# Moving value, weight and key/query loads of a fused attention + MLP kernel to earlier slots

## The chip, the cores and the metric

One core of a Trainium2 chip. Its engines are PE (TensorE, with its weight loads shown apart as PEld), DVE (VectorE), ACT (ScalarE), POOL (GpSimd) and SP (SyncE, which only issues transfers). They run side by side, each through its own instructions in order, and wait for each other by semaphores. The metric is the device time of the whole program in microseconds (us), the median of several runs.

## The reference

Attention over 8 batches of 8 heads, 576 rows, 64 columns, and then a two-layer MLP over the 4608 rows of 512:

```python
scores = scale * np.matmul(q, k.transpose(0, 1, 3, 2))
thresh = np.max(scores, axis=-1, keepdims=True) - tau
scores = np.where(scores >= thresh, scores, -1000000000.0)
attn = np.exp(scores - max); attn = attn / (sum + 1e-09)
x = matmul(attn, v), heads side by side, as (4608, 512)
h = x @ w_in                       # 512 x 2048
out = (h * np.clip(h + 3.0, 0.0, 6.0) / 6.0) @ w_out   # 2048 x 512
```

(max and sum are those of the row; the last lines of the attention are put together here.)

## The kernel before

**Tiling.** Two heads make a pair and two pairs a *quad*; there are 16 quads, two per batch. A quad has 9 *slots*: eight of 128 query rows of one pair (both its heads), and one that takes the last 64 rows of both pairs. The loop of L527 runs over the 144 slots n; quad q has slots 9q to 9q + 8. Each pass n works on several slots at once (a pipeline written out by hand), and each engine takes the pass's work in the order of the code:

- `scores(n+2)` (L277): PE makes q times k into PSUM, for both heads.
- `sm_max(n+1)` (L294): DVE copies scores out of PSUM and takes the row maximum (L302); POOL turns it into the mask's bias (L305).
- `sm_mask`, `sm_exp` (L307, L312): ACT applies the threshold (L309) and the exponential with row sum (L314). Up to slot N1 = 22 the exponential of slot n-1 stands ahead of the mask of slot n.
- `sm_recip(n-1)` (L316): DVE takes the reciprocal of the row sums (L317).
- `sm_norm(n-1)` (L319): POOL scales the rows to bf16 (`pn`, L322). They are transposed either by PE (`pe_transpose`, L337, two passes later, for the slots marked `on_chip`: slots before 21 with number 1, 3, 5, 7 or 8 in their quad, and number 0 from quad 1 on), or by a DMA transpose that SP issues (L330).
- `multiply(n)`: PE multiplies transposed rows with values (L346, L349). From slot 22 on PE also has the MLP's two matmuls (L381, L415), with ACT (L389) and DVE (L391, L404) between them.

PE also has filler: transposes of the identity (`warm_up`, L185), 17 at the start, some more in the lead-in, and 8 + 6 per pass in passes 0 to 7.

**Loads.** `load_quad(quad)` (L82) allocates a quad's tiles from a pool of three buffers (L49) and appends its transfers as jobs to the list `loads`. For the first two batches (quads 0 to 3) these are five jobs: keys of pair 0, queries of pair 0, remainders (last 64 rows of keys and queries, four transfers), keys of pair 1, queries of pair 1, all issued by SP (except the first queries, by ACT). From quad 4 on there are four jobs: queries 0, keys 0, queries 1, and `both`, which is the key remainders and keys 1. These transfers are cut into 32-row blocks, four per job, issued by SP; the key remainders are issued by POOL:

```python
(nc.sync if b < NB else nc.gpsimd).dma_start(out=dst[64 * n:64 * n + 64, :]...   # L126, n = 0, 1
```

`load_v(b)` (L138) appends a batch's value transfers to `vcasts` (two of four heads each and two remainders for batches 0 and 1), and `load_weights` (L161) appends 16 pieces of w_in and then 16 of w_out to `casts`; POOL issues these, since they change f32 into bf16 on the way.

**When they are issued.** `start(jobs, n)` (L171) pops and issues up to n jobs. Quad 0 is issued ahead of everything (L176). The others come at the end of each pass, behind `sm_norm` (L618 to L625): first one job of `loads` in most passes, then either one of `vcasts` or one or two of `casts`, by the pass's number. L535 says in which pass a quad's jobs are appended to `loads`.

**The lead-in** (L452 to L480) is the work before the loop: PE transposes the first keys (L232) and queries (L458 to L461), and makes the scores of slots 0 and 1; DVE and POOL make the maximum and the bias of slot 0.

Of the kernel before, what the change touches and what calls it, by code (L numbers as in the profile page):

```python
# [9 lines left out]
F32 = mybir.dt.float32  # L10
# [5 lines left out]
P = 128  # L16
# [4 lines left out]
def kernel(  # L21
# [10 lines left out]
    nc = tc.nc  # L32
# [15 lines left out]
    singles = ctx.enter_context(tc.tile_pool(name="singles", bufs=1))  # L48
# [20 lines left out]
    nat = {}  # L69
# [6 lines left out]
    loads = []  # L76
    casts = []
    vcasts = []
# [59 lines left out]
    def load_v(b):  # L138
        vm = v_pool.tile([P, H, 4 * D], BF16, tag="vm", name="vm")
        vr = vrs[b % 2]  # L140
        vsb[b] = (vm, vr)
        w = 4 if b < NB else 2
        mains = [lambda h=h: nc.gpsimd.dma_start(  # L143
            out=vm[:, h:h + w, :], in_=v[b, h:h + w, 0:512, :].rearrange("h (p t) d -> p h (t d)", t=4))
            for h in range(0, H, w)]
        rests = [lambda a=a: nc.gpsimd.dma_start(
            out=vr[a * 64:(a + 1) * 64, a, :, :],
            in_=v[b, :, 512:S, :].rearrange("(hp a) p d -> a p hp d", a=2)[a]) for a in range(2)]
        vcasts.extend(mains + rests if b < NB else mains[0:1] + rests + mains[1:])
# [21 lines left out]
    def start(jobs, n):  # L171
        for _ in range(min(n, len(jobs))):
            jobs.pop(0)()
# [9 lines left out]
    def warm_up(count):  # L183
        for _ in range(count):
            nc.tensor.transpose(ps[:, HB, 0:P], identf[:], identf[:])  # L185

    warm_up(17)
    identb = singles.tile([P, P], BF16)
    nc.vector.tensor_copy(out=identb[:], in_=identf[:])
    three = singles.tile([P, 1], F32)  # L190
# [103 lines left out]
    def sm_max(sl):  # L294
        sl.s = s_pool.tile([P, 2, S], F32, tag="s", name="s")
        sl.m = stat_pool.tile([P, 2], F32, tag="m", name="m")
        sl.bias = stat_pool.tile([P, 2], F32, tag="bias", name="bias")
        sl.rsum = stat_pool.tile([P, 2], F32, tag="rsum", name="rsum")
        sl.rinv = stat_pool.tile([P, 2], F32, tag="rinv", name="rinv")
        for i in range(2):  # L300
            c0 = score_col(sl.n, i)
            nc.vector.tensor_scalar(out=sl.s[:, i, :], in0=ps_flat[:, c0:c0 + S],  # L302
                                    scalar1=1.0, scalar2=None, op0=Alu.mult, op1=Alu.max,
                                    accum_out=sl.m[:, i:i + 1])
        nc.gpsimd.tensor_scalar(out=sl.bias[:], in0=sl.m[:], scalar1=-scale, scalar2=tau, op0=Alu.mult, op1=Alu.add)  # L305

    def sm_mask(sl, i):  # L307
        s = sl.s[:, i, :]
        nc.scalar.activation(out=s, in_=s, func=Act.Prelu, bias=sl.bias[:, i:i + 1], scale=scale,  # L309
                             alpha=REJECT)  # L310

    def sm_exp(sl, i):  # L312
        s = sl.s[:, i, :]
        nc.scalar.activation(out=s, in_=s, func=Act.Exp, accum_out=sl.rsum[:, i:i + 1])  # L314

    def sm_recip(sl):  # L316
        nc.vector.reciprocal(out=sl.rinv[:], in_=sl.rsum[:])  # L317
# [54 lines left out]
    def mm1(item, hb=HB):  # L372
        b, ni, c0 = item
        if c0 is None:
            for ki in range(KI):
                nc.tensor.matmul(ps[:, hb, :], xR[b // 2][:, ki, :], w_in_sb[:, ki, ni * P:ni * P + 512],  # L376
                                 start=(ki == 0), stop=(ki == KI - 1))
        else:
            for n in range(2):
                for ki in range(KI):  # L380
                    nc.tensor.matmul(ps[:, hb, n * 256:(n + 1) * 256], w_in_sb[:, ki, (ni + n) * P:(ni + n + 1) * P],  # L381
                                     xT[b][:, ki, c0:c0 + 256], start=(ki == 0), stop=(ki == KI - 1))
        return ps[:, hb, :]
# [122 lines left out]
    def multiply(n):  # L506
        copies = []
        for of, pair, *columns in products.get(n, ()):
            copies.append(av_rest(of) if pair is None else av_main(pair, *columns))
            if of % 2 and pair is None:  # L510
                todo1.extend(moe_of(of // 2)[1])
            elif pair == 2 * of + 1 and of % 2 and columns[0] == 0:
                todo1.extend(moe_of(of // 2)[0])
        return copies

    def second():
        nonlocal pieces, bb, mt, part
        pieces = 2 if now % 2 == 0 and todo2 else 0
        for _ in range(pieces):
            bb, mt, part = todo2.pop(0)  # L520
            mm2_part(bb, mt, part)
# [5 lines left out]
    for n, sl in enumerate(queue):  # L527
        quad, slot = sl.quad, sl.slot
        b, g = divmod(quad, 2)
        now = n  # L530
        if slot in (0, 4):
            pts[2 * quad + slot // 4] = pt_pool.tile([P, 9, 512], BF16, tag="pT", name="pT")
        if slot == 8:
            ptr[quad] = ptr_pool.tile([P, 9, P], BF16, tag="pR", name="pR")
        for ahead in {0: (1, 2), 9: (3,), 16: (4,)}.get(n, (quad + 2,) if quad > 2 and slot == (2 if quad == 3 else 0) else ()):  # L535
            if ahead < NQUAD:
                load_quad(ahead)
        if slot == 0 and g == 1 and b + 1 < B:
            load_v(b + 1)
        for copy in last_keys:  # L540
            copy()
        last_keys = []
        if 0 < n <= N1:
            for i in range(2):
                sm_exp(prev, i)
        if n + 1 < len(queue):
            sm_max(queue[n + 1])
        even = n >= N1 and n % 2 == 0
        if n > N1:
            sm_recip(prev)  # L550
        for copy in waiting:
            copy()
        waiting = []

        if todo1:
            item, then = todo1.pop(0)
            if n == len(queue) - 2:
                second()
            h = mm1(item, 0 if n == len(queue) - 1 else OB if n > N1 and n % 2 and not pieces else HB)
            todo2.extend(then)  # L560
        else:
            item = None
        if n >= N1:
            for copy in multiply(n):
                copy()
        if item:
            mm1_gate(item, h, mm1_relu(h, on_act=even))
        copies = pe_transpose(queue[n - 2]) if n > 1 and queue[n - 2].on_chip else None
        if prev is not None and n < N1:
            sm_recip(prev)  # L570
        if copies:
            copies()
        if n != len(queue) - 2:
            second()
        if n <= N1:
            for i in range(2):
                sm_mask(sl, i)
        if n == N1:
            sm_recip(prev)
        if n >= N1:  # L580
            for i in range(2):
                sm_exp(sl, i)
            if n + 1 < len(queue):
                for i in range(2):
                    sm_mask(queue[n + 1], i)
        if n < N1:
            for copy in multiply(n):
                copy()
        if part == 3:
            waiting.append(lambda tile=(bb, mt): late.extend(mm2_out(*tile, on_act=False)))  # L590
            part = 0
        evict = []
        for job, of in turns.get(n, ()):
            if job == "k":
                (last_keys if even else evict).append(transpose_k(of))
            elif job == "q":
                if of // 2 not in qkT:
                    alloc_qk(of // 2)
                (waiting if even else evict).append(transpose_q(of))
            else:  # L600
                (last_keys if even else evict).append(transpose_rest(of, of_k=of > 0))
        for out_of_psum in evict:
            if out_of_psum:
                out_of_psum()
        if n == 0:
            warm_up(8)
        if n <= N1:
            scores(n + 2)
        elif n % 2:
            for m in (n + 3, n + 2):  # L610
                if m < len(queue):
                    scores(m)
        if n < 8:
            warm_up(6)
        if n > 0:
            sm_norm(prev)
        flush()
        if n == 0:  # L618
            start(loads, 2)
        elif n not in (4, 12, 15, 18, 21) and not 23 < n < 30 and (n < 37 or n % 2 == 0):  # L620
            start(loads, 1)
        if n < 4 or 15 < n < 20 or n > 33:
            start(vcasts, 1 if n < N1 or n % 2 else 0)
        else:
            start(casts, 2 if n in (5, 8, 11, 14) or 21 < n < 28 else 1)  # L625
        prev = sl
# [82 lines left out]
```

## Time and profile before

| what | value |
|---|---|
| median of 8 runs | 520.68 us (519.96 to 521.04) |
| the profiled execution | 520.73 us, span 519.0 us |
| PE busy | 503.6 us, 97% of the span |
| DVE, ACT, POOL busy | 442.6, 452.1, 299.3 us |
| DMA | 78.77 MB, mean 152 GB/s |
| queue q1 (SP's transfers) and q0 (POOL's), share of 16 engines | 77.3% and 15.2% |
| lead-in, up to the first mask on ACT | 10.8 us |

The span is what lies between the first and the last instruction on record; the time is what the device took for the program. Times inside the profile count from the span's start. A pass is found in the trace by POOL's bias (L305): the first of its 144 lies in the lead-in, and the k-th after it in pass k - 1. So passes 0 to 21 lie at 10.8 to 76.6 us, and the steady stage, in which two passes take some 6.3 us together, begins near 116 us. Idle time in front of an instruction is given in square brackets, with what ended it; "issue" means that the profile shows nothing that it waited for.

### The profile page before, as it was taken

The numbers are of one execution on the slowest core, as the hardware profiler recorded it, in microseconds if no ns is written. First come the engines' busy times: TensorE is split into PE (matmuls) and PEld (weight loads), VectorE is DVE, ScalarE is ACT, GpSimd is POOL, SyncE is SP. The second block draws the span as 40 slices with busy tenths as digits, with TensorE's granted clock in tenths as the row PEclk, the third lists the DMA queues.
The fourth block names the chain that finished last, engine by engine and source line by source line (L and its number), as shares of the span: only waits on it lengthen the run. The fifth ranks groups of instructions, "written<-read, shape, count | busy, mean of one in ns | idle before, by whom it ended". The sixth has DMA issues, their size and how long they took to land.

```text
span 519.0 us, 12068 instructions
## 1 busy us (share of the span) xinstructions
PE 503.6 (97%) x4089; PEld 321.8 (62%) x4145; DVE 442.6 (85%) x1124; ACT 452.1 (87%) x980; POOL 299.3 (58%) x538
## 2 busy tenths in 40 slices
PE   8999899999999999999999999999999999999997
PEld 6765555666665666666665666666665666667563
DVE  3788887998999999999999999999999999887261
ACT  3999979999999999999999999999999999987060
POOL 0787869756676666657566656657566655552000
PEclk9999999999999999999999999999999999999999
DMA  5799899989999999999999999999999997564222
GB/s 131 111 176 167 138 157 162 171 150 174 166 175 156 166 171 161 171 161 175 174 157 188 155 192 169 163 168 176 168 155 185 178 177 122 117 112 70 78 66 61
DMA packets 314094, 78.77 MB, mean 152 GB/s; under 512 B 296624, under 2 KB 309168, under 8 KB 314032
## 3 DMA queue, kind: packets, MB, share of 16 engines
q1 hardware_dynamic: 294464, 67.90, 77.3%
q0 software_dynamic: 18368, 9.71, 15.2%
q8 instruction: 32, 0.52, 0.5%
q10 hardware_dynamic: 1200, 0.39, 0.3%
q14 instruction: 30, 0.25, 0.1%
HBM read 36.70 MB, written 9.44 MB: 89 GB/s over the span
## 4 chain that ended last, share of the span: by engine, by line
PE 80%; ACT 3%; DVE 2%; issue 1%; POOL 0%; POOLq 0%
PE ps L287 25%; PE ps L415 23%; PE ps L381 21%; PE ps L346 6%; PE ps L376 3%; ACT s L314 1%; PE ps L349 1%; ACT s L309 1%; DVE g L404 1%; ACT r L389 1%; DVE s L302 0%; DVE r L391 0%; POOL pn L322 0%; PE ps L257 0%; ACT kT L222 0%
## 5 line engine op out<-in xcount | busy, mean ns | idle before, releaser
L322 POOL TENSOR_SCALAR pn<-s,rinv 128x576 bf16<-128x576 f32 x288 | 210.6, 743 | 19.9 <-issue 4.5
L302 DVE TENSOR_SCALAR_CACHE_REDUCE s<-ps 128x576 f32<-128x576 f32 x288 | 205.0, 749 | 17.6 <-PE ps L287 9.0
L309 ACT ACTIVATE s<-s,bias 128x576 f32<-128x576 f32 x288 | 205.8, 763 | 6.0 <-POOL bias L305 5.7
L314 ACT ACTIVATE s<-s 128x576 f32<-128x576 f32 x288 | 192.5, 671 | 0.3
L287 PE MATMUL ps<-kT,qT 64*128 64x384 f32 (+7 forms) x1280 | 174.0, 419 | 4.7 <-DVE s L302 3.8
L287 PEld LDWEIGHTS ps<-kT,qT 64*128 64x128 f32 (+1 forms) x1280 | 103.6, 175 | 59.3 <-issue 15.8
L381 PE MATMUL ps<-xT,w_in_sb 128*128 128x256 bf16 x1024 | 130.9, 273 | 0.2 <-DVE g L404 0.2
L415 PE MATMUL ps<-w_out_sb,g 128*128 128x512 bf16 x524 | 123.7, 379 | 2.8 <-issue 0.2
L381 PEld LDWEIGHTS <-w_in_sb 128*128 128x128 bf16 x1024 | 95.5, 98 | 40.0 <-issue 20.8
L305 POOL TENSOR_SCALAR bias<-m 128x2 f32<-128x2 f32 x144 | 26.9, 187 | 154.3 <-DVE rinv L317 137.1
L404 DVE SCALAR_TENSOR_TENSOR g<-r,ps 128x512 bf16<-128x512 f32 x128 | 87.8, 687 | 15.1 <-ACT r L389 11.1
L415 PEld LDWEIGHTS <-g 128*128 128x128 bf16 x576 | 56.2, 98 | 56.8 <-issue 0.4
L389 ACT ACTIVATE r<-ps,three 128x512 f32<-128x512 f32 x81 | 55.6, 687 | 27.9 <-PE ps L381 23.8
L314 ACT ACTIVATION_READ_ACCUMULATOR s<-s 128x1 f32 x288 | 54.5, 189 | 0.0
L391 DVE TENSOR_SCALAR r<-ps 128x512 f32<-128x512 f32 x63 | 42.9, 681 | 0.0
L346 PE MATMUL ps<-pT,vm 128*64 128x256 bf16 (+1 forms) x480 | 39.1, 285 | 0.0
L346 PEld LDWEIGHTS <-vm 128*64 128x64 bf16 x736 | 27.2, 110 | 16.0 <-issue 14.3
L357 DVE CAST xT<-ps 128x256 bf16<-128x256 f32 (+1 forms) x60 | 26.2, 437 | 11.8 <-PE ps L349 11.8
L423 DVE TENSOR_SCALAR osb<-ps 128x512 f32<-128x512 f32 x31 | 20.9, 673 | 8.4 <-PE ps L415 8.4
L302 DVE DVE_READ_ACCUMULATOR s<-ps 128x1 f32 x288 | 23.9, 83 | 0.0
L317 DVE RECIPROCAL rinv<-rsum 128x2 f32<-128x2 f32 x144 | 23.0, 160 | 0.6 <-ACT s L314 0.6
L143 POOL DMA_DIRECT2D vm<-in_v_dram x28 | 21.4, 766 | 0.7 <-issue 0.7
(57 smaller groups left out, 260.5 us busy)
## 6 DMA issues: line engine op xcount, KB each, us to landing
out_dram<-osb SPq DMA_DIRECT2D x31, 256.0 KB, 3.4
nq<-in_q_dram SPq DMA_DIRECT2D x96, 72.0 KB, 3.5
km<-in_k_dram SPq DMA_DIRECT2D x96, 64.0 KB, 3.1
vm<-in_v_dram POOLq DMA_DIRECT2D x24, 128.0 KB, 4.1
km<-in_k_dram SPq DMA_DIRECT2D x16, 128.0 KB, 3.5
w_in_sb<-in_moe_w_in_dram POOLq DMA_DIRECT2D x16, 128.0 KB, 3.6
w_out_sb<-in_moe_w_out_dram POOLq DMA_DIRECT2D x16, 128.0 KB, 3.9
pT<-pn SPq DMA_TRANSPOSE x117, 3.8
```

What stands on the lines that cost most here:

```text
L287: nc.tensor.matmul(ps_flat[rows, c0:c0 + w], qT_of(pair)[a * 64:(a + 1) * 64, q0:q0 + rows.stop - rows.start], kT_of(pair)[a * 64:(a + 1) ...
L302: nc.vector.tensor_scalar(out=sl.s[:, i, :], in0=ps_flat[:, c0:c0 + S], scalar1=1.0, scalar2=None, op0=Alu.mult, op1=Alu.max, accum_out=sl ...
L305: nc.gpsimd.tensor_scalar(out=sl.bias[:], in0=sl.m[:], scalar1=-scale, scalar2=tau, op0=Alu.mult, op1=Alu.add)
L309: nc.scalar.activation(out=s, in_=s, func=Act.Prelu, bias=sl.bias[:, i:i + 1], scale=scale, alpha=REJECT)
L314: nc.scalar.activation(out=s, in_=s, func=Act.Exp, accum_out=sl.rsum[:, i:i + 1])
L322: nc.gpsimd.tensor_scalar(out=pn[:, i, :], in0=sl.s[:, i, :], scalar1=sl.rinv[:, i:i + 1], scalar2=1.0, op0=Alu.mult, op1=Alu.mult)
L346: nc.tensor.matmul(pb[a * 64:(a + 1) * 64, :], vm[:, 2 * hp + a, c * D:(c + 1) * D], pT[:, 5 * a + c, cols], start=(c == 0), stop=False)
L381: nc.tensor.matmul(ps[:, hb, n * 256:(n + 1) * 256], w_in_sb[:, ki, (ni + n) * P:(ni + n + 1) * P], xT[b][:, ki, c0:c0 + 256], start=(ki = ...
L389: nc.scalar.activation(out=r, in_=hps, func=Act.Relu, bias=three[:])
L391: nc.vector.tensor_scalar(out=r, in0=hps, scalar1=3.0, scalar2=0.0, op0=Alu.add, op1=Alu.max)
L404: nc.vector.scalar_tensor_tensor(out=out, in0=r, scalar=6.0, in1=hps, op0=Alu.min, op1=Alu.mult)
L415: nc.tensor.matmul(o_ps[0], gbuf[:, ni, mt * P:(mt + 1) * P], w_out_sb[:, ni, :], start=(ni == 0), stop=(ni == NI - 1))
```

## The change

```diff
     warm_up(17)
+    landed = singles.tile([P, 1], F32)
+    nc.gpsimd.tensor_copy(out=landed[:], in_=nat[0][1][:, 0, 1, 0:1])
+    start(vcasts, 2)
+    start(casts, 3)
...
-        for ahead in {0: (1, 2), 9: (3,), 16: (4,)}.get(n, ...):
+        for ahead in {0: (1, 2), 6: (3,), 13: (4,)}.get(n, ...):
...
         if n == 0:
-            start(loads, 2)
+            start(loads, 5)
...
-        if n < 4 or 15 < n < 20 or n > 33:
+        if n < 2 or 15 < n < 20 or n > 33:
             start(vcasts, 1 if n < N1 or n % 2 else 0)
```

In the lead-in POOL copies one column of the first pair's second key tile, and so waits for that transfer; then it issues two value transfers (four heads each) and three w_in pieces. Pass 0 issues all five jobs of quad 1 (12 transfers of SP in place of 4). Following the lists through the code, the jobs fall into the passes like this (k, q, r: keys, queries, remainders; the digit is the pair, then the quad; w: w_in piece, wo: w_out piece; v: values of batch 0):

| pass | before: SP | before: POOL | after: SP | after: POOL |
|---|---|---|---|---|
| lead-in | quad 0 | | quad 0 | v, v, 3 w |
| 0 | k0.1 q0.1 | v | k0.1 q0.1 r.1 k1.1 q1.1 | v rest |
| 1 | r.1 | v | k0.2 | v rest |
| 2 | k1.1 | v rest | q0.2 | w |
| 3 | q1.1 | v rest | r.2 | w |
| 5 to 9 | quad 2 | 7 w | k1.2, q1.2 (5, 6), k0.3 q0.3 r.3 | 7 w |
| 10 to 16 | quad 3 | 8 w, v of batch 1 | k1.3 q1.3 (10, 11), q0.4 (13) k0.4 (14) q1.4 (16) | 3 w, 5 wo, v of batch 1 |
| 17 | q0.4 | v of batch 1 | k1.4 | two key remainders of quad 4, v of batch 1 |
| 19, 20 | k0.4, q1.4 | v of batch 1 (19), wo (20) | | the same |
| 22 | k1.4 | two key remainders of quad 4, 2 wo | | 2 wo |
| 26 to 29 | | 6 wo | | 1 wo (26) |

From pass 30 on nothing changes. The number of value and weight pieces in passes 0 to 25 is the same in both; in passes 2 and 3 weight pieces take the place of value pieces.

More of the change, by code (lines that the diff above doesn't have):

```diff
@@ L534 @@
             ptr[quad] = ptr_pool.tile([P, 9, P], BF16, tag="pR", name="pR")
-        for ahead in {0: (1, 2), 9: (3,), 16: (4,)}.get(n, (quad + 2,) if quad > 2 and slot == (2 if quad == 3 else 0) else ()):
+        for ahead in {0: (1, 2), 6: (3,), 13: (4,)}.get(n, (quad + 2,) if quad > 2 and slot == (2 if quad == 3 else 0) else ()):
             if ahead < NQUAD:
```

## The prediction

> **What bounds the kernel now.** I read the view by windows first, with the borders put where the code changes its schedule. A row gives the stretch, then busy time (and instructions) of PE, PEld, DVE, ACT and POOL, the granted clock, the DMA share and GB/s:
>
> ```profile
> 10.80:76.60 65.80, 61.78 (x496) 40.39 (x496) 54.23 (x149) 59.92 (x132) 49.84 (x90) 1.00 0.94 146
> 76.60:116.40 39.80, 37.60 (x333) 24.91 (x335) 35.30 (x93) 38.80 (x86) 29.69 (x54) 1.00 1.06 162
> 116.40:470.00 353.60, 350.80 (x2931) 222.44 (x2982) 329.99 (x841) 333.83 (x732) 217.29 (x385) 1.00 1.02 164
> ```
>
> From 116.4 on PE is busy 350.8 of 353.6 us, and the change moves nothing there. From 76.6 to 116.4 ACT is busy 38.8 of 39.8. From 10.8 to 76.6 (passes 0 to 21) PE's 61.78 includes 56 filler transposes, so I ask the view of waits what is late there (total, times, longest):
>
> ```profile
> POOL bias L305 <- DVE rinv L317: 10.3, 19, 1.3
> PEld L337 <- POOL pn L322: 5.9, 18, 0.5
> ACT s L309 <- POOL bias L305: 5.7, 6, 3.3
> ```
>
> The engines wait for each other in a ring. DVE makes the maximum, POOL the bias and the normalised rows, PE transposes those rows (L337) before the next scores, and ACT masks with the bias. No wait in this stretch names a load. In the chain that ended last, POOL is a link:
>
> ```profile
> 70.31 0.09 DVE rinv L317
> ...
> 70.43 0.17 POOL bias L305
> 70.61 0.08 issue
> 70.69 1.47 POOL pn L322 x2
> 72.16 0.05 issue
> 72.21 0.45 PE ps L337 x5
> ```
>
> So time on POOL in passes 0 to 21 can cost, and an earlier load as such gains nothing.
>
> **1. POOL in the lead-in.** The tiny copy (the 128x2 bias row takes 0.19) waits for the second key transfer, whose first reader, L232 on PE, starts at 5.18. Then come two value issues (L143: 0.74 to 0.93) and three weight issues (L164: 0.54 to 0.60): 0.19 + 1.49 to 1.86 + 1.61 to 1.79 = 3.3 to 3.8 us, from 5.2 to 8.5 to 9.0. POOL's next work, the first bias, starts at 10.57 after 9.25 us idle. Cost nothing, with 1.5 us of cover. If the issues took 1.5 us more, each further us would delay the first mask.
>
> **2. The DMA engines in the lead-in.** These five transfers now run beside the first quad's second keys and queries, which SP issues from 4.8 to 7.4. How the queues share is seen at 63.5 to 65.0, where both have work:
>
> ```profile
> q0 software_dynamic: 340, 0.17, 86.1%
> q1 hardware_dynamic: 338, 0.09, 43.7%
> ```
>
> One packet each in turn, 225 a us per queue. Alone, SP's queue moved 4113 from 6.5 to 11.5, 823 a us. The first value transfer was issued at 13.27 and its packets ran in earnest from 14.9, so here from about 6.9. By then SP's queue has done 0.4 us x 823 = 330 of the 2048 packets that the second queries need. The 1024 value packets take 1024/225 = 4.6 us, the 384 weight packets 2.4 us (78 beside 81 of SP's in the 0.5 us from 60.0): 13.9 us, and 1738 of SP's are through. The last 310 take 0.4, the receipt 0.5: 14.7 us. At the sharing of 67.0 to 67.9 (310 against 296 in 0.9 us) it is 13.3. The first reader, L232 in pass 1, starts at 14.87. So nothing is lost, by 0.2 to 1.6 us; I take 0. Keys, remainders and the second quad come later (first use 17.36, 21.16, 23.58). The remainder of the first keys and queries has landed by 6.2, before the value packets start.
>
> The Trainium skill, page "DMA: Bandwidth & Descriptors", section "Issuing engines are not separate DMA queues", speaks against this part: DMAs of all issuers run on the same 16 engines and interleave, so a further issuer saves only issue time. By its fit (section "Anatomy of one DMA", 2.0 us + bytes/436e3) the 1.84 MB would be through 6.2 us after issue, near 11.5 as an estimate, and the sum stays as it is.
>
> **3. SP.** Pass 0 issues 12 transfers instead of 4. The eight more at 0.6 to 0.65 each keep SP from 9.8 to 14.9; its next work, the first DMA transpose, waits for pn until 17.30. Cover 2.4 us; without it, that transpose's first reader is L346 at 34.84. Cost 0. The jobs of quads 2 and 3 then move up by 2 to 3 passes, one a pass as before. Quad 4's move from passes 17, 19, 20, 22 to 13, 14, 16, 17. There the old order held one transpose back: the rows of pass 23 were ready at 83.94, SP came to them at 84.85, behind four key blocks. That goes; but the first to read them is L346 at 97.40, so the gain is 0.
>
> **4. POOL in pass 17: the cost.** Quad 4's last job issues four key blocks on SP and also the two key remainders on **POOL** (L126). Before it lies in pass 22, at 79.72, 1.28 us; now it comes in pass 17, behind pn and ahead of a value issue. POOL in passes 17 and 18:
>
> ```profile
> 61.62 0.18 POOL L305 TENSOR_SCALAR bias<-m 128x2 f32<-128x2 f32 x1
> 61.89 1.47 POOL L322 TENSOR_SCALAR pn<-s,rinv 128x576 bf16<-128x576 f32 x2
> 63.30 0.80 POOL L143 DMA_DIRECT2D vm<-in_v_dram  x1
> 64.28 0.18 POOL L305 TENSOR_SCALAR bias<-m 128x2 f32<-128x2 f32 x1 [0.18 <-DVE rinv L317]
> 64.55 1.47 POOL L322 TENSOR_SCALAR pn<-s,rinv 128x576 bf16<-128x576 f32 x2
> ```
>
> The only spare time is 0.18 us, of which some 0.1 is there between back-to-back instructions too (63.30 + 0.80 to 64.28, against 60.74 + 0.80 to 61.62). So bias and pn of pass 18 come 1.28 - 0.10 = 1.18 late. Three ways lead on:
> - ACT: its mask starts at 64.62, 0.34 after the bias starts; now the bias starts at 65.46 and the mask 0.22 later (the distance from 70.41 to 70.63), 65.68: 1.06 late. In pass 21 ACT waits 0.50 anyway (at 70.63), so of this alone 0.56 would be left.
> - PE: it already waits for this very pn:
>
> ```profile
> 66.07 0.45 PE L337 MATMUL ps<-identb,pn 128*128 128x128 bf16 x5 [0.26 <-POOL pn L322]
> ```
>
>   L337, the two L232 groups and the scores at 67.33 follow one another without a hole, so the scores start at 68.51.
> - DVE: a maximum follows its scores' start by 1.35 (64.24 to 65.59). 68.51 + 1.35 = 69.86 instead of 68.88, **0.98 late**. The mask of pass 21, which waits for DVE through the bias, is late by the same, and so is the chain above, through L346 to the mm1 of pass 22, for which ACT waits 3.2 us, the longest wait of the stage.
>
> The second and third agree within 0.2; what reaches the chain is DVE's 0.98, and after 76.6 ACT has no hole to win it back. Bounds: 0 if the issue were free; 1.28 if nothing absorbs. I take **+0.98**.
>
> The Trainium skill, same page, section "Anatomy of one DMA", has a dispatch of some 50 ns and descriptor generation that is "small, variable". The two issues would then cost about 0.1, as an estimate, the 0.1 of slack would hide them, and the sum would be no change. The row of L126 (24 issues, 0.61 to 0.66) decides.
>
> **5. What POOL is relieved of.** Passes 0 to 3 issue smaller pieces: 0.93 to 0.65, 0.80 to 0.65, twice 0.65 to 0.58. POOL idles 1.32 and 0.20 before the next biases: 0. Pass 22 loses its 1.28 and passes 26 to 29 lose five w_out issues, 5 x 0.57 = 2.9 us. There POOL has no hole (78.31 to 89.65), but ACT in 76.6 to 116.4 waits for L381 alone, 4.0 us in two waits, and never for POOL. Gain 0; at most the 39.8 - 38.8 = 1.0 us in which ACT is idle.
>
> **Sum.** The profiled execution took 520.73 (span 519.0, 1.7 around it), 0.05 above the median 520.68. 520.73 + 0.98 = **521.7 us**, +0.19%. About 0.2%, or 1.04 us, is what a measurement of this kernel tells from no change, so the forecast lies at that edge.
>
> **Rivals.**
> - *Absorbed.* The issue in pass 17 meets slack that I have not weighed rightly (ACT's 0.50 in pass 21, POOL's idle 0.53 and 0.95 in passes 19 and 20), and nothing else moves: 0 to +0.3, 520.8. For it: POOL has those holes. Against: PE waits for pn before them. 2 in 10.
> - *The lead-in's transfers are late as well.* The queues share worse than in step 2, and the queries of pass 1 land 0.5 to 1.2 after 14.87. L232, the scores at 15.40 and the maximum at 16.67 have no hole, so that it adds in full: 521.7 + 0.8 = 522.5. For it: the slow end of step 2 leaves 0.2. Against: the quick end leaves 1.6. 1.5 in 10.
> - *Faster.* POOL, not ACT, sets the pace after pass 22: it is busy 8.1 of the 8.9 us from 82.2 to 91.1, without a hole. This decides if the stall of pass 17 is absorbed and POOL's lateness there is what stretches ACT's sequence; then the relief of step 5 gives up to 1.0: 519.7. Against: ACT is busy 8.85 of the same 8.9. 1.3 in 10.
> - *Forecast*, 521.2 to 522.1: 5.2 in 10.
>
> **Chances and range.** Half of the forecast's cases lie above the 0.2% mark (PE's 1.18, or a copy dearer than its row, push up): 2.8 slower, 2.4 within. Late transfers are all slower, absorbed all within, faster all faster: faster 0.13, within 0.44, slower 0.43. The range leaves out the better half of *faster* and the worse half of the late transfers: 520.1 to 522.7.
>
> **What would show it.** Right: POOL's rows of pass 17 show kr x2 between pn and vm, the next bias starts near 65.5 by the old clock, ACT's wait for the bias has a new entry of about 1.0, and passes 22 on are the same, shifted. Step 2 is wrong if L232 of pass 1 waits; step 5 is wrong if the stretch from the first mm1 to the steady stage is shorter than 39.8. The prediction is wrong as a whole if the ring of passes 18 to 21 takes as long as before.

## The result and the profile after

The changed kernel takes 522.44 us (median of 10 runs, 522.13 to 522.75), the kernel before 520.34 in the 28 runs beside it (519.78 to 521.04): ratio 1.0039, 95% interval 1.0031 to 1.0047. It is slower by 2.1 us. The profiled execution took 522.39 (span 520.6), 1.66 more than the one of before.

In the changed kernel the lines from L189 on have moved down by four (L302 is now L306, L232 is L236, and so on). Here are the same stretches as in the prediction, with borders moved by what the chain moved (stretch, then busy time of PE, PEld, DVE, ACT, POOL, the clock, DMA share, GB/s):

```profile
10.80:78.30 67.50, 61.62 (x500) 40.13 (x499) 54.49 (x149) 60.05 (x133) 50.63 (x92) 1.00 1.03 160
78.30:118.10 39.80, 37.54 (x333) 24.90 (x334) 35.31 (x93) 38.84 (x86) 25.79 (x47) 1.00 0.87 136
118.10:471.70 353.60, 350.82 (x2932) 222.46 (x2983) 329.97 (x841) 333.93 (x732) 217.53 (x385) 1.00 1.00 164
```

The second and third are as long as before, to 0.1 us, although POOL is busy 3.9 us less in the second. All of the loss lies in the first, passes 0 to 21. The view of waits for it says whose (total, times, longest):

```profile
POOL bias L309 <- DVE rinv L321: 10.3, 16, 1.6
PEld L341 <- POOL pn L326: 7.3, 18, 1.3
ACT s L313 <- POOL bias L309: 7.2, 8, 3.3
```

PE's wait for pn has grown from 5.9 to 7.3, its longest from 0.5 to 1.3; ACT waits for the bias twice more. Where this happens is read from POOL's biases (L305, now L309), one for each slot: I subtract their times before from those after. The difference is nothing up to the third bias, jumps by 0.67 at the fourth (pass 2), stays at 0.65 to 0.68 up to pass 17, jumps again at the bias of pass 18 (1.82), and settles at 1.64 by pass 20. In passes 23 to 27, where POOL has been relieved, it dips to as little as 0.35; from pass 28 on it is 1.62 to 1.66 to the end. What POOL wins there is gone again. So there are **two places**, 0.67 and 0.97.

**Second place, pass 17.** POOL's instructions in passes 17 and 18 after:

```profile
62.57 1.46 POOL L326 TENSOR_SCALAR pn<-s,rinv 128x576 bf16<-128x576 f32 x2
63.98 1.27 POOL L126 DMA_DIRECT2D kr<-in_k_dram  x2
65.25 0.78 POOL L143 DMA_DIRECT2D vm<-in_v_dram  x1
66.10 0.18 POOL L309 TENSOR_SCALAR bias<-m 128x2 f32<-128x2 f32 x1
66.38 1.46 POOL L326 TENSOR_SCALAR pn<-s,rinv 128x576 bf16<-128x576 f32 x2
```

The two key remainders stand between pn and the value issue, and the bias behind them has no idle time any more. ACT waits for that bias with a new entry of about 1.0, as the prediction said, and PE stands still for the pn, where it waited 0.26 before:

```profile
66.32 1.44 ACT L313 ACTIVATE s<-s,bias 128x576 f32<-128x576 f32 x2 [0.94 <-POOL bias L309]
67.18 0.40 PE L341 MATMUL ps<-identb,pn 128*128 128x128 bf16 x4 [1.02 <-POOL pn L326]
67.90 0.45 PE L341 MATMUL ps<-identb,pn 128*128 128x128 bf16 x5 [0.33 <-POOL pn L326]
```

**First place, pass 1.** The queries that PE transposes there come late, with a wait that the profile of before does not have:

```profile
15.51 0.63 PE L236 MATMUL ps<-identf,nq 128*128 128x128 f32 x4 [0.50 <-DMA nq<-in_q_dram]
```

It started at 14.87 before. What POOL's queue (q0) and SP's (q1) got in the microsecond from 7.0 to 8.0, after:

```profile
DMA packets 133, 0.06 MB, mean 57 GB/s; under 512 B 37, under 2 KB 133, under 8 KB 133
## 3 DMA queue, kind: packets, MB, share of 16 engines
q0 software_dynamic: 96, 0.05, 72.0%
q1 hardware_dynamic: 37, 0.01, 5.2%
```

and before, in the same microsecond:

```profile
q1 hardware_dynamic: 731, 0.18, 80.0%
```

The two queues together moved far less than SP's alone had (133 packets against 731), so taking turns does not explain it. It happens while POOL's queue gets under way: its first packets started at 6.93. That queue starts slowly by itself, too: in the kernel before, with SP's queue silent, it moved 161 packets from 15.0 to 16.0 and 286 in the microsecond after.

The chain that ended last goes through the same links as before, 1.64 us later:

```profile
71.95 0.09 DVE rinv L321
...
72.05 0.20 POOL bias L309
72.25 0.09 issue
72.33 1.47 POOL pn L326 x2
73.80 0.05 issue
73.85 0.45 PE ps L341 x5
```

### The profile page after: what moved, and what is told of

It reads as the page before. It is cut to its first block, busy times and chain, and to the rows that moved or that the text cites. A ratio compares the mean times of both kernels' runs of the same rounds, so it can differ in the third digit from the quotient of the medians.

```text
span 520.6 us, 12064 instructions
## 1 busy us (share of the span) xinstructions
PE 503.3 (97%) x4088; PEld 321.5 (62%) x4145; DVE 442.8 (85%) x1124; ACT 452.3 (87%) x980; POOL 299.8 (58%) x539
## 4 chain that ended last, share of the span: by engine, by line
PE 80%; ACT 3%; DVE 2%; issue 1%; POOL 0%
PE ps L291 25%; PE ps L419 23%; PE ps L385 21%; PE ps L350 6%; PE ps L380 3%; ACT s L318 1%; PE ps L353 1%; ACT s L313 1%; DVE g L408 1%; ACT r L393 1%; DVE s L306 0%; DVE r L395 0%; POOL pn L326 0%; PE ps L261 0%; ACT kT L226 0%
## 5 line engine op out<-in xcount | busy, mean ns | idle before, releaser
L306 DVE TENSOR_SCALAR_CACHE_REDUCE s<-ps 128x576 f32<-128x576 f32 x288 | 205.1, 749 | 17.8 <-PE ps L291 7.9
L309 POOL TENSOR_SCALAR bias<-m 128x2 f32<-128x2 f32 x144 | 26.9, 187 | 152.8 <-DVE rinv L321 136.5
L306 DVE DVE_READ_ACCUMULATOR s<-ps 128x1 f32 x288 | 23.9, 83 | 0.0
```

## The experiments

Theory: two separate costs. POOL's issues in pass 17 hold back bias and pn (0.97), and POOL's pieces in the lead-in hold back the second queries (0.67 in this profile). Rivals: the earlier transfers of SP crowd the DMA engines (for either place); POOL's issues, not the transfers, delay the lead-in; and for the end, that POOL's relief in passes 22 to 29 gives something back. The table gives the distances between biases, in us (bias k is that of slot k), which leave out how long the lead-in took (bold: where they differ from before). Each ratio is against runs of the kernel before beside it, whose medians are 520.34 (after), 520.36 (e1 to e4), 520.38 (e5 to e9) and 520.27 (e10, e11):

| kernel | bias 0 at | 0 to 3 | 3 to 18 | 18 to 21 | 21 to 32 | median, ratio (95%) |
|---|---|---|---|---|---|---|
| before | 10.57 | 7.65 | 43.41 | 8.79 | 35.45 | 520.34 |
| after | 10.55 | **8.33** | 43.42 | **9.75** | 35.45 | 522.44, 1.0039 (1.0031 to 1.0047) |
| e1 remainders by SP | 10.21 | **8.56** | 43.42 | 8.79 | 35.45 | 521.95, 1.0029 (1.0020 to 1.0037) |
| e2 no lead-in pieces | 10.14 | 7.65 | 43.40 | **9.74** | 35.45 | 521.31, 1.0018 (1.0009 to 1.0028) |
| e3 lead-in alone | 9.83 | **9.23** | 43.42 | 8.78 | 35.45 | 521.61, 1.0020 (1.0010 to 1.0031) |
| e4 remainders alone | 9.72 | 7.65 | 43.40 | **9.74** | 35.45 | 521.21, 1.0015 (1.0006 to 1.0024) |
| e5 queries first | 9.85 | 7.63 | 43.43 | **9.75** | 35.44 | 521.21, 1.0020 (1.0011 to 1.0030) |
| e6 values alone | 10.53 | 7.63 | 43.41 | **9.75** | 35.44 | 521.58, 1.0016 (1.0007 to 1.0024) |
| e8 SP's loads alone | 9.80 | 7.65 | 43.39 | 8.78 | 35.45 | 520.29, 1.0000 (0.9992 to 1.0009) |
| e9 masks first | 10.97 | 7.65 | 43.40 | 8.79 | **34.79** | 520.25, 1.0002 (0.9984 to 1.0021) |
| e10 e9, remainders by SP | 10.61 | 7.65 | 43.42 | 8.79 | **34.47** | 520.21, 0.9995 (0.9986 to 1.0004) |
| e11 all of it | 10.94 | 7.63 | 43.42 | 8.79 | **34.45** | 519.30, 0.9984 (0.9974 to 0.9995) |

**e1: quad 4's key remainders by SP.**

```diff
-                    (nc.sync if b < NB else nc.gpsimd).dma_start(
+                    (nc.sync if b < NB or quad == 4 else nc.gpsimd).dma_start(
```

> The changed kernel, but SP issues the two key remainders of quad 4 in pass 17 instead of POOL. Theory (POOL's issue time of 1.27 us in pass 17 makes bias and pn of pass 18 late): the second step goes, the bias of pass 18 lies 0.66 behind the kernel before like those around it, and the time is 1.0 below the changed kernel, +0.7 over the kernel before. Rival (the earlier key and query transfers of quads 3 and 4 crowd the DMA engines, and who issues the remainders does not matter): the step of 0.97 stays, +1.6.

The second jump is gone (18 to 21: 8.79) with the same transfers, which SP now issues from 66.69 where POOL issued them from 63.98. So it is the issue on POOL and not the traffic. The median, 1.59 above the kernel before, is higher than I expected (0.7). The first jump is 0.9 in this profile, not 0.67, and a second hole opens in the steady stage: at 184.52 PE waits 0.30 for a DMA transpose, after which all is 0.36 later. PE has that wait in no other profile but e10's, which has two of the kind (0.5 in all). These two kernels issue quad 4's remainders from SP, but so do e8 and e11, which do not have it; why it comes was not settled.

**e2: no pieces in the lead-in** (the four lines taken out, `n < 2` back to `n < 4`).

> The changed kernel without the copy and the five pieces in the lead-in; the values are issued in passes 0 to 3 again, and the weights follow as in the kernel before. Theory (the pieces' packets take turns with the first quad's second queries, which land after PE wants them in pass 1): the step of 0.66 in pass 2 goes, the step of 0.97 at pass 18 stays, +1.0 over the kernel before. Rival (the eight more transfers that SP issues in pass 0 are what crowds the queries): the first step stays, +1.6.

0 to 3 is 7.65 again and 18 to 21 stays 9.74: theory, with +0.95 in the medians. SP's eight more transfers in pass 0 do no harm.

**e3: the lead-in alone** (the kernel before with those four lines and `n < 2`).

> The kernel before with the copy and the five pieces in the lead-in as the only change; the loads of SP stay where they were. Theory: the first step alone, L236 of pass 1 starts near 15.5 instead of 14.9, +0.7 over the kernel before. Rival (SP's eight more transfers): no step, +0.0. Rival of a gain (five pieces fewer in passes 26 to 29 set POOL free): below +0.5, with the distance shrinking between 93 and 105 us.

Only the first jump appears, but of 1.6, not 0.67, and the median is 1.25 above the kernel before, not 0.7. The reason is in its lead-in: PE was ready earlier, and the queries were not:

```profile
13.42 0.88 PE L185 MATMUL ps<-identf 128*128 128x128 f32 x6
15.70 0.63 PE L236 MATMUL ps<-identf,nq 128*128 128x128 f32 x4 [1.40 <-DMA nq<-in_q_dram]
```

The last query transfer landed at 15.37 after, 15.27 in e1 and 15.56 in e3 (9.55 to 9.87 in the kernels without pieces), while bias 0 lay at 10.55, 10.21 and 9.83. So this landing is, to 0.3 us, a **fixed date**: whatever the lead-in gains, pass 1 waits for it. 21 to 32 is unchanged, which rules out the rival of a gain.

**e4: the remainders alone** (the kernel before; `both` of quad 4 without `rest`, which is called at `n == 17` behind `sm_norm`).

> The kernel before, with the two key remainders of quad 4 issued by POOL in pass 17 instead of 22 as the only change. Theory: nothing up to pass 17, then one step of 0.97 in the bias of pass 18 that stays to the end, +1.0 over the kernel before. Rival (the issue is absorbed by the holes of passes 19 to 21, and it is the DMA traffic of the other loads that made the step): up to 0.3.

One jump, +0.95 on 18 to 21, and nothing else: this edit alone carries the second place. Median +0.85.

**e5: queries first.** In the order of quad 0 the second queries go ahead of the second keys.

```diff
-            loads.extend((lambda: load_k(0), lambda: load_q(0), rest, lambda: load_k(1), lambda: load_q(1)))
+            jobs = [lambda: load_k(0), lambda: load_q(0), rest, lambda: load_k(1), lambda: load_q(1)]
+            loads.extend(jobs if quad else jobs[0:3] + jobs[4:] + jobs[3:4])
```

> The changed kernel, with SP issuing the first quad's second queries ahead of its second keys; all else stays, POOL's pieces in the lead-in too. Theory (SP's queue moves at half or less beside POOL's, and what stands second in it lands near 15.5): the queries land near 11, L236 of pass 1 waits for nothing; the keys land near 15.5, a pass ahead of their reader. The step of pass 2 goes and the step of pass 18 stays: +0.9 over the kernel before. Rival (POOL's issues themselves delay the lead-in): the step stays, +2.0.

The queries landed at 10.37, the keys at 15.88. In order of time, PE in passes 1 and 2:

```profile
14.15 0.60 PE L237 MATMUL ps<-identf,nq 128*128 128x128 f32 x4
...
16.65 0.60 PE L237 MATMUL ps<-identf,km 128*128 128x128 f32 x4
```

No wait for the queries, and 0 to 3 is 7.63, with all of POOL's issues still in the lead-in. The landing is the cause, and its price was a matter of order. The median is 0.83 above the kernel before, as expected.

**e6: two value pieces alone** (without `start(casts, 3)`).

> The changed kernel with the two value pieces alone in the lead-in; the three w_in pieces come in the passes, so that the weights end with pass 29 as in the kernel before. Theory (each packet of POOL's queue lets one of SP's through): the queries land some 2 us earlier, near 13.3, before the reader at 14.0 to 14.9; no step in pass 2, +0.9 over the kernel before. Rival (the value packets alone, or the 7 to 8 us in which both queues nearly stand still, are enough): a step of 0.3 or more.

The queries landed at 13.78, a little later than I expected, and no jump is seen. But here bias 0 lay at 10.53; with an early lead-in (reader at 14.0) 0.2 would be left, so values alone are on the edge. The median is 1.2 above the kernel before, more than the 0.9 expected: the eleven runs fall into two groups, 520.84 to 521.03 and 521.58 to 522.04, and the median is the lowest of the second. The fastest run is level with that of e5 (520.81).

**e8: SP's earlier loads alone** (e1 and e2 together).

> The changed kernel without the lead-in pieces and with the key remainders of quad 4 issued by SP: what is left of the change is that SP's loads of quads 1 to 4 come earlier. Theory: no load was late, so none of this moves the end: 0.0 to +0.3 over the kernel before. Rival of a loss (the earlier transfers crowd the DMA transposes): above +0.5. Rival of a gain (SP free for the transposes of passes 21 to 25, POOL relieved of 1.27 us in pass 22): below -0.5.

All distances are those of before to 0.02, and the ratio is 1.0000: earlier key and query loads are worth nothing, and cost nothing.

**e9: masks first.** The chain of waits had shown ACT idle for 3.2 us in pass 22, with a bias ready, behind a relu. In the kernel before, with the later copies of these calls left out for that pass:

```diff
+        if n == N1:
+            for i in range(2):
+                sm_mask(sl, i)
+            for i in range(2):
+                sm_exp(sl, i)
         if item:
             mm1_gate(item, h, mm1_relu(h, on_act=even))
```

> The kernel before, with ACT's masks and exponentials of slot 22 ahead of the first relu of pass 22, so that they fill the 3.2 us for which ACT waits for PE there. If ACT sets the pace from 76.6 to 116.4, as the forecast had it when it gave POOL's relief there no gain, the time falls by what PE can follow: PE waits 2.2 us in that stretch, so -1.0 to -2.2. Rival (PE and DVE set the pace after pass 22 and ACT merely keeps up): 0.0 to -0.3.

The wait for mm1 falls from 3.2 to 0.57, but 21 to 32 shrinks by 0.66 only, and the median does not tell it from nothing. The time went into a new wait, behind POOL's key remainders and weight pieces of pass 22:

```profile
82.82 1.44 ACT L309 ACTIVATE s<-s,bias 128x576 f32<-128x576 f32 x2 [1.61 <-POOL bias L305]
```

So ACT is not alone in setting the pace there. The median, 520.25 against 520.38, lies in the rival's range; the 0.66 of the profile lies between the rival's and mine.

**e10: e9, and quad 4's remainders by SP.**

> The kernel before with the masks of slot 22 ahead of the relu (as in e9) and with the key remainders of quad 4 issued by SP in their old place, pass 22. With the masks first, ACT had a new wait of 1.6 us for the bias that POOL computes at 82.6, behind the two key remainders and two w_out pieces. Theory (the same as in pass 17: POOL's issue time counts where the bias behind it is waited for): that wait falls by 1.27 to some 0.3. PE's mm1 of pass 23 starts no sooner, so of the time only 0.3 to 0.5 is won over e9, -1.0 to -1.5 against the kernel before. Rival (the wait is DVE's, not POOL's): it stays at 1.6.

ACT's wait for the bias falls to 0.5 in two, and 21 to 32 by another 0.32: theory for the wait.

```profile
ACT s L309 <- POOL bias L305: 0.5, 2, 0.3
```

The time missed what I expected: the median, 520.21, is 0.06 below the kernel before, not 1.0 to 1.5. The profile loses 0.5 again to two late DMA transposes, as in e1. The fastest run, 518.95, is 0.9 below the fastest of the kernel before beside it (519.88), which is about what 21 to 32 won; but the twelve runs spread over 2.6 us, and why they do was not settled.

**e11: everything** (the changed kernel with e1, e5 and e9, and one w_out piece instead of two in pass 22).

> The changed kernel with queries first in quad 0, quad 4's key remainders issued by SP, the masks of slot 22 ahead of the relu, and one w_out piece instead of two in pass 22 (the lead-in's pieces make room for that). Theory: no step in pass 2 and none in pass 18; the wait for the bias in pass 23 goes wholly, by 1.6; -1.0 to -1.6 against the kernel before, like e10, since the change's own parts are worth nothing once they cost nothing. Rival (the pieces moved into the lead-in free POOL where it counts): below e10 by 0.5 or more.

No jump in either place, and 21 to 32 is 34.45, as in e10. ACT's wait for the bias is down to 0.2. By the medians the rival would hold, since 519.30 is 0.9 below e10; but the fastest runs are level (519.01 and 518.95), and the two profiles differ only behind bias 32 (359.61 and 360.30 us from there to the last bias), where e10 has its late transposes. So nothing shows that the pieces moved into the lead-in give more. At 519.30 this is the lowest median of the study, 1.0 below the kernel before and 3.1 below the changed one.

## Why the prediction was right, and where it was not

The direction was right, and 522.44 lies inside 520.1 to 522.7. The forecast of 521.7 was 0.7 low, and the time is that of the rival whose transfers in the lead-in are late as well (522.5). The forecast had one of the two costs; the time lies in the range because the range took in the better half of that rival.

1. **POOL in the lead-in**: right. Its copy starts at 5.13 and its last issue ends at 8.57 (8.5 to 9.0 predicted); the first bias did not move.
2. **The DMA engines in the lead-in**: the step that failed. It had the second queries land at 13.3 to 14.7; they landed at 15.37, 0.5 after the reader wanted them. Equal turns did come (179 and 180 packets from 8.0 to 9.0, 358 and 356 from 12.0 to 14.0), at some 180 a us each and not 225. Before that both queues nearly stood still: 133 packets in the microsecond from 7.0, 37 of them SP's, for which I had counted 225 of SP's alone. And the sum took the 16 engines as equally fast. Without POOL's pieces the first and the last of them finished this transfer 0.7 us apart (8.94 and 9.63), here 2.8 us (12.59 and 15.37, 14.54 in the mean). How much of the lateness is the spread differs: in e1 they finished only 0.9 apart (14.41 to 15.27, 14.89 in the mean), and the transfer was as late. The 0.5 us for the receipt comes from no row of the prediction; in four kernels without the pieces (before, e4, e9, e10) the last landing came 0.3 to 0.4 behind the end of the last packet. The prediction's other estimate, 11.5 for the five transfers, was further off: the last of them landed at 15.70. The other end of the comparison was taken as fixed, too: the reader's 14.87 is that of one execution. Bias 0 lies anywhere from 9.72 to 10.97 in the profiles of this study.
3. **SP**: no cost, as forecast (e8, and e5 with POOL's pieces beside them), but not for the reason given. SP was not done by 14.9; its issues stretched to 20.6 and the first DMA transpose moved from 17.30 to 20.74, past the cover of 2.4 us. What held was the second line: the first reader came at 34.84, and comes at 35.5 now without a wait.
4. **POOL in pass 17**: right in mechanism and size, 0.98 forecast and 0.97 measured (0.95 alone in e4). Bias and pn of pass 18 were late by 1.15 against the passes before (1.18 forecast), and DVE's slack took the rest. The row of L126 (0.61 to 0.66 an issue) decided rightly against the small dispatch cost that the Trainium skill gives (page "DMA: Bandwidth & Descriptors", section "Anatomy of one DMA").
5. **POOL's relief**: right, 21 to 32 is the same to 0.01 us in after, e1 to e8. That ACT sets the pace there was only half the reason: e9 took 2.7 us of waiting from ACT and won 0.66.

**The sum.** The two places make 0.67 + 0.97 = 1.64, and the spans differ by 1.6. The medians differ by 2.1. With one edit each, e3 and e4 stand 1.25 and 0.85 above the kernel before in their medians, 2.1 together: the first place costs more in the medians than in this one pair of profiles. That fits step 2: the profile of before (520.73) was 0.4 above its own median, an execution with a late lead-in. The changed kernel waits for the same date in any case, so it does not have the early ones: bias 3 lies at 18.78 to 19.07 in after, e1 and e3, and at 17.37 to 18.62 in the others, and the runs spread over 0.6 us instead of 1.3. That the runs without a profile differ by their lead-ins is argued from these, not shown.

## What to carry to other kernels

An issue on an engine that also computes is an instruction like any other: count its time against the slack of the instruction behind it, in the very pass into which it is moved, and not over the stage. When transfers are started earlier, look for the one already in flight that is needed first, work out its landing with the slowest engine and with the start of the other queue in it, and put it first in its queue (e5: the whole cost of the first place, for a change of order). A load that no wait names gains nothing by coming earlier (e8).

## What the runs showed of the hardware that I had not expected

**PE's rate in the lead-in differs from run to run.** The four transposes of the first keys, and the four fillers behind them, in the profile of before:

```profile
5.21 1.09 PE L232 MATMUL ps<-identf,km 128*128 128x128 f32 x4
6.09 0.86 PE L185 MATMUL ps<-identf 128*128 128x128 f32 x4
```

and the same instructions in e4:

```profile
5.04 0.63 PE L237 MATMUL ps<-identf,km 128*128 128x128 f32 x4
5.51 0.60 PE L190 MATMUL ps<-identf 128*128 128x128 f32 x4
```

At 5.95 instead of 6.79 PE comes to the first queries, and bias 0 lies 0.85 earlier. The windows' clock column reads 1.00 in the stretches 0 to 5.0 and 5.0 to 10.8 of before, but it counts time without a record as full, and the trace's first record of the granted clock, at full, starts at 6.62 in before and at 4.80 in e4. In all 12 profiles that record starts between 4.09 and 7.44, and within 0.25 us of it PE's starts go from 0.21 to 0.11 us apart. Bias 0 goes with it: 9.72 to 9.85 in the four profiles whose record starts before 5.3, and from 10.14 (record at 5.95) to 10.97 (7.44) in the others. So the late lead-ins are those in which the full clock was granted late, in kernels with and without the change. The Trainium skill, page "TensorE: Matmul & The Clock Gate", section "Part 1: The HAM clock gate", has PE start at half rate and go to full rate after some 3.4 us of work, at a moment that varies from run to run. The rows agree in that the starts come twice as fast, and in that the moment varies: 2.7 to 6.1 us after PE's first instruction (1.37).

**A second queue does not start for nothing.** In the first microsecond of POOL's packets SP's queue fell from 731 packets to 37 (after), 49 (e1), 33 (e6) and 74 (e3). In e5 and e11 POOL's packets came later, from 7.2 on, and SP's queue had 123 and 110 from 7.5 to 8.5. In the changed kernel the two then took equal turns (179 and 180 packets from 8.0 to 9.0). What stands still in SP's queue no run tells.
